# The top-32 threshold of attention rows from folded halves: scans of 288 columns in place of 576

## Chip, cores, metric

The kernel runs on one core of one Trainium2 chip. The time is that of the device in microseconds; three runs of the kernel before gave 2672.0, 2672.44 and 2674.5, median 2672.44.

## What is computed

Attention over 8 batches, 8 heads, 576 tokens and head width 64, in which each row of scores keeps only its 32 largest; then a mixture of experts (top 1 of 8) on the 4608 rows of 512.

```python
scores = scale * np.matmul(q, k.transpose(0, 1, 3, 2))
kth = np.partition(scores, -top_k, axis=-1)[..., -top_k:-top_k + 1]     # top_k = 32
scores = np.where(scores >= kth, scores, -1e9)
attn = np.exp(scores - np.max(scores, axis=-1, keepdims=True))
attn = attn / (np.sum(attn, axis=-1, keepdims=True) + 1e-09)
x = np.matmul(attn, v)                       # rows to (4608, 512)
expert_idx = np.argmax(x @ w_gate, axis=1)   # and its softmax weight gate_w
# rows sorted by expert:  y = relu(x @ w1[e]) @ w2[e];  out = gate_w * y
```

All data is float32.

## The kernel before

There are two stages. The first is attention with routing, the second the experts' blocks.

The first stage walks over 32 units (b, u): a batch and a pair of heads. A unit has nine score tiles of 128 query rows by 576 keys: four per head, and one that holds the last 64 rows of both heads. They are worked in five groups: `(i, NC + i)` for i = 0 to 3, which is the same rows of the two heads, and the ninth tile alone. For each tile `scores` makes 576 columns in two PSUM halves of 288 (PE, L182) and ACT copies them to `s` (L188; four buffers for all tiles). `weights` then finds the 32nd largest of each row on DVE: four times MAX8 (the eight largest of a row, L200) and between them three match_replace (L205), which overwrite those eight with -3e38. After the first MAX8, POOL makes `nbias` from the largest (L202) and ACT the exponentials `ex` (L203). One scalar_tensor_tensor (STT, L212) multiplies `ex` by `s >= 32nd value` into `w` (three buffers) and sums each row to `z`. `transposed` turns `w` on PE (L223, L224; the `wTl` tile has one PSUM buffer) and ACT copies the result to `wT`, `wTt` (L228, L229). When a unit's ninth tile is done, `outputs` multiplies by v in two halves of the queries (`po`, L253), ACT copies them to `oT` (L254), PE turns them back (`px`, `pl`), and DVE writes them, divided by `z`, into `x` (L262, L269; two buffers). After every eighth unit `route` finds the expert of 1152 tokens, writes their numbers to lists and `x` to `x_rows` in DRAM.

The code issues `scores` one group ahead of `weights`, and `finish` one tile behind. The order on each engine's queue is then chosen by a scheduler over the whole program; each engine works through its own queue in order, and a row that waits holds all behind it. In that order the scans of two neighbouring tiles are interleaved on DVE.

The second stage runs 25 blocks of 256 rows through the experts (L431 to L464). It doesn't depend on how the threshold was found.

Of the kernel before, what the change touches and what calls it, by code (L numbers as in the profile page):

```python
# [1 line left out]

# [28 lines left out]
def kernel(  # L31
# [9 lines left out]
):  # L41

# [90 lines left out]
    cnt = None  # L133
    firstp = ctx.enter_context(tc.tile_pool(name="firstp", bufs=1))
    first_w = None

    with (
        tc.tile_pool(name="pad", bufs=1) as padp,
        tc.tile_pool(name="load", bufs=2) as load,
        tc.tile_pool(name="att", bufs=2) as att,  # L140
        tc.tile_pool(name="wtp", bufs=2) as wtp,
        tc.tile_pool(name="xp", bufs=2) as xp,
        tc.tile_pool(name="small", bufs=3) as small,
        tc.tile_pool(name="ps_s", bufs=2, space=bass.MemoryType.PSUM) as ps_s,
        tc.tile_pool(name="ps_w", bufs=2, space=bass.MemoryType.PSUM) as ps_w,
        tc.tile_pool(name="ps_1", bufs=1, space=bass.MemoryType.PSUM) as ps_1,
    ):
        qk, vs_of, xt, units = {}, {}, {}, {}

        def load_qk(b, u):  # L150
            qb = load.tile([P, 2, S], F32, name="qb")
            nc.sync.dma_start(qb, qt[b, u * P:(u + 2) * P, :].rearrange("(u p) s -> p u s", p=P))
            kb = load.tile([P, 2, S], F32, name="kb")
            nc.sync.dma_start(kb, kt[b, u * P:(u + 2) * P, :].rearrange("(u p) s -> p u s", p=P))
            for n in range(2):
                qk[b, u + n] = (qb[:, n, :], kb[:, n, :])

        def load_v(b):
            vb = load.tile([P, KC, HD], F32, name="vb")
            nc.sync.dma_start(vb[:, 0:NC, :], vt[b, 0:SM, :].rearrange("(c p) d -> p c d", p=P))  # L160
            nc.sync.dma_start(vb[0:ST, NC, :], vt[b, SM:S, :])
            vs_of[b] = vb

        def parts(i):

            if i < 2 * NC:
                h, c = divmod(i, NC)
                return [(h, slice(0, P), slice(c * P, (c + 1) * P))]
            return [(h, slice(h * ST, (h + 1) * ST), slice(SM, S)) for h in range(2)]

        def scores(b, u, tiles):
            qu, ku = qk[b, u]
            todo = []
            got = []
            for i in tiles:
                ps = ps_s.tile([P, 2, SM], F32, name="sc")
                todo += [(ps, h, rows, cols) for h, rows, cols in parts(i)]
                got.append(ps)
            for j in range(2):
                for ps, h, rows, cols in todo:  # L180
                    d = slice(h * D, (h + 1) * D)
                    nc.tensor.matmul(  # L182
                        ps[rows, j, 0:HF], qu[d, cols], ku[d, j * HF:(j + 1) * HF], start=True, stop=True
                    )
            out_s = []
            for ps in got:
                s = att.tile([P, 2, HF], F32, name="s", bufs=4)
                nc.scalar.copy(s, ps[:, :, 0:HF])  # L188
                out_s.append(s)
            return out_s  # L190

        def weights(b, u, i, s3):
            s = s3[:, :, :].rearrange("p j k -> p (j k)")
            tops = small.tile([P, TOP_K // 8, 8], F32, name="tops")
            scr = att.tile([P, S], F32, name="scr")
            nbias = small.tile([P, 1], F32, name="nbias")
            ex = att.tile([P, S], F32, name="ex")
            src = s
            for r in range(TOP_K // 8):
                nc.vector.max(out=tops[:, r, :], in_=src)  # L200
                if r == 0:
                    nc.gpsimd.tensor_scalar(nbias, tops[:, 0, 0:1], -scale, None, ALU.mult)  # L202
                    nc.scalar.activation(ex, s, AF.Exp, scale=scale, bias=nbias)  # L203
                if r < TOP_K // 8 - 1:
                    nc.vector.match_replace(  # L205
                        out=scr, in_to_replace=tops[:, r, :], in_values=src, imm_value=NEG
                    )
                    src = scr
            w = att.tile([P, S], F32, name="w", bufs=3)
            z = units[b, u][2]  # L210
            c = 2 * NC if i == 2 * NC else 2 * (i % NC) + i // NC
            nc.vector.scalar_tensor_tensor(  # L212
                out=w, in0=s, scalar=tops[:, TOP_K // 8 - 1, 7:8], in1=ex,
                op0=ALU.is_ge, op1=ALU.mult, accum_out=z[:, c:c + 1],
            )
            return w

        def transposed(b, u, i, w):
            wT, wTt, _ = units[b, u]
            pm = ps_w.tile([P, NC, P], F32, name="wTm")  # L220
            pt = ps_1.tile([P, SM], F32, name="wTl")
            for c in range(NC):
                nc.tensor.transpose(pm[:, c, :], w[:, c * P:(c + 1) * P], ident)  # L223
# [291 lines left out]
```

## Time and profile before

| what | value |
|---|---|
| profiled execution | 2672.9 us, span 2671.2 us |
| PE busy | 2038.4 us (76%) |
| DVE busy | 1736.8 us (65%) |
| ACT busy | 718.1 us (27%) |
| POOL busy | 199.7 us (7%) |
| granted TensorE clock, mean | 0.719 of 2.4 GHz |

The shares are means over the two stages, which have different limits: in the first, to about 1850 us, DVE is the busiest engine, in the second PE. So they must be read by stage. A busy PE is counted from records whose ends are modelled; the time from one start to the next is surer. The clock is granted at two levels, 1.2 GHz (0.50) and 2.4 GHz (1.00); numbers between are means over a stretch.

### The profile page before, as it was taken

What the parts mean: (1) busy time and instruction counts of PE and PEld (TensorE: products, weight loads), DVE (VectorE), ACT (ScalarE), POOL (GpSimd) and SP (SyncE); (2) the same over time, 40 slices, a digit from 0 to 9 for tenths busy, and PEclk for the clock granted to TensorE, in tenths of its full rate; (3) what the DMA queues carried; (4) which work ended last, traced back from release to release, by engine and by line L of the source; (5) the groups of instructions that cost most, each with busy time, mean ns of one, the idle gap of its engine ahead of it and who ended that gap; (6) DMA issues with size and microseconds to landing.
All of it is one profiled execution on the core that took longest, in us unless ns stands there. A gap on an engine that the chain in (4) does not pass through costs nothing. (4 is left out here: it accounts for less than half of the span.)

```text
span 2671.2 us, 22208 instructions
## 1 busy us (share of the span) xinstructions
PE 2038.4 (76%) x7208; PEld 1205.5 (45%) x7208; DVE 1736.8 (65%) x3864; ACT 718.1 (27%) x1457; POOL 199.7 (7%) x453
## 2 busy tenths in 40 slices
PE   5766677666776876677686677676199999999998
PEld 3333344433333543333353333334166666666665
DVE  8999999699999869999986999995100010010000
ACT  3333333233333323333332333332011011001100
POOL 0000000100000010000001000000111111111110
PEclk8666656566656655655666656665599999999999
DMA  3000001100000110000011000000364444545440
GB/s 136 18 18 19 18 1 36 36 18 18 18 18 0 36 36 18 18 18 18 0 36 36 18 18 0 1 0 0 118 224 162 177 175 178 181 159 198 158 154 2
DMA packets 71172, 166.84 MB, mean 62 GB/s; under 512 B 9612, under 2 KB 9740, under 8 KB 71058
## 3 DMA queue, kind: packets, MB, share of 16 engines
q1 hardware_dynamic: 61906, 142.83, 15.8%
q0 software_dynamic: 9152, 22.60, 2.2%
q8 instruction: 58, 0.95, 0.1%
q14 instruction: 56, 0.46, 0.1%
HBM read 146.34 MB, written 22.73 MB: 63 GB/s over the span
## 5 line engine op out<-in xcount | busy, mean ns | idle before, releaser
L223 PE MATMUL wTm<-ident,w 128*128 128x128 f32 x1152 | 282.1, 392 | 490.1 <-DVE w L212 473.2
L200 DVE MAX8 tops<-scr 128x8 f32<-128x576 f32 x864 | 620.1, 744 | 0.5
L182 PE MATMUL sc<-kb,qb 64*128 64x288 f32 (+1 forms) x1280 | 575.2, 654 | 33.1 <-ACT s L188 26.0
L223 PEld LDWEIGHTS wTm<-ident,w 128*128 128x128 f32 x1152 | 187.7, 198 | 667.3 <-issue 498.9
L205 DVE MATCH_REPLACE8 scr<-tops,scr 128x576 f32<-128x576 f32 x576 | 424.9, 738 | 0.0
L182 PEld LDWEIGHTS sc<-kb,qb 64*128 64x128 f32 (+1 forms) x1280 | 279.2, 269 | 205.4 <-issue 109.7
L452 PE MATMUL ph<-xTs,w 128*128 128x256 f32 x1600 | 353.8, 382 | 14.1 <-DVE xTs L447 13.5
L188 ACT COPY s<-sc 128x576 f32<-128x576 f32 x288 | 184.3, 640 | 640.9 <-DVE w L212 632.7
L459 PE MATMUL py<-w,hT 128*128 128x512 f32 x800 | 347.4, 592 | 0.0
L452 PEld LDWEIGHTS ph<-xTs,w 128*128 128x128 f32 x1600 | 303.4, 191 | 60.4 <-DVE xTs L447 19.0
L463 DVE TENSOR_SCALAR y<-py,xg 128x512 f32<-128x512 f32 x50 | 37.5, 751 | 441.7 <-PE py L459 441.7
L253 PE MATMUL po<-wT,vb 128*64 128x288 f32 x1024 | 277.5, 642 | 1.4 <-ACT wT L228 0.9
L455 ACT ACTIVATE hT<-ph 128x256 f32<-128x256 f32 x200 | 76.8, 384 | 701.6 <-PE ph L452 701.6
L203 ACT ACTIVATE ex<-s,nbias 128x576 f32<-128x576 f32 x288 | 223.8, 777 | 94.0 <-POOL nbias L202 93.7
L459 PEld LDWEIGHTS py<-w,hT 128*128 128x128 f32 x800 | 152.0, 190 | 180.7 <-issue 179.4
L212 DVE SCALAR_TENSOR_TENSOR w<-s,tops,ex 128x576 f32<-128x576 f32 x288 | 230.1, 800 | 1.1 <-ACT ex L203 0.9
L200 DVE MAX8 tops<-s 128x8 f32<-128x576 f32 x288 | 213.7, 744 | 8.0 <-ACT s L188 7.9
L205 DVE MATCH_REPLACE8 scr<-tops,s 128x576 f32<-128x576 f32 x288 | 212.5, 738 | 0.0
L228 ACT COPY wT<-wTm 128x512 f32<-128x512 f32 x256 | 150.1, 586 | 171.3 <-PE wTm L223 168.1
L202 POOL TENSOR_SCALAR nbias<-tops 128x1 f32<-128x1 f32 x288 | 60.8, 211 | 1664.3 <-DVE tops L200 1393.5
L253 PEld LDWEIGHTS po<-wT,vb 128*64 128x64 f32 x1024 | 108.6, 213 | 163.4 <-issue 157.5
L431 DVE TENSOR_SCALAR src<-idx 128x2 int32<-128x2 int32 x25 | 4.2, 169 | 261.2 <-DMA idx<-lists 261.2
(89 smaller groups left out, 981.1 us busy)
## 6 DMA issues: line engine op xcount, KB each, us to landing
w<-in_moe_w_dram SPq DMA_DIRECT2D x50, 2048.0 KB, 11.2
qb<-in_qt_dram SPq DMA_DIRECT2D x16, 576.0 KB, 4.0
kb<-in_kt_dram SPq DMA_DIRECT2D x16, 576.0 KB, 4.9
x_rows<-x SPq DMA_DIRECT2D x8, 1026.0 KB, 10.7
vb<-in_vt_dram SPq DMA_DIRECT2D x8, 1024.0 KB, 5.9
x_rows<-x SPq DMA_DIRECT2D x8, 128.2 KB, 10.6
vb<-in_vt_dram SPq DMA_DIRECT2D x8, 128.0 KB, 6.1
xg<-x_rows,src POOLq DMA_INDIRECT x50, 7.7
```

The lines of the kernel that those rows point to most:

```text
L182: nc.tensor.matmul(ps[rows, j, 0:HF], qu[d, cols], ku[d, j * HF:(j + 1) * HF], start=True, stop=True)
L188: nc.scalar.copy(s, ps[:, :, 0:HF])
L200: nc.vector.max(out=tops[:, r, :], in_=src)
L203: nc.scalar.activation(ex, s, AF.Exp, scale=scale, bias=nbias)
L205: nc.vector.match_replace(out=scr, in_to_replace=tops[:, r, :], in_values=src, imm_value=NEG)
L212: nc.vector.scalar_tensor_tensor(out=w, in0=s, scalar=tops[:, TOP_K // 8 - 1, 7:8], in1=ex, op0=ALU.is_ge, op1=ALU.mult, accum_out=z[:, c: ...
L223: nc.tensor.transpose(pm[:, c, :], w[:, c * P:(c + 1) * P], ident)
L228: nc.scalar.copy(wT[:, :, h, q], pm)
L253: nc.tensor.matmul(po[rows, 0:HF], lhsT, rhs, start=(c == 0), stop=(c == KC - 1))
L452: nc.tensor.matmul(ph, w1[:, 0, dt, f * P:(f + 1) * P], xT[:, dt, :], start=(dt == 0), stop=(dt == DT - 1))
L455: nc.scalar.activation(hT[:, f, :], ph, AF.Relu)
L459: nc.tensor.matmul(py, hT[:, f, c * P:(c + 1) * P], w2[:, 0, f, :], start=(f == 0), stop=(f == FT - 1))
```

## The change

Columns j and j + 288 of a row of scores are taken as a pair. `hl[:, 0, :]` is the larger of each pair and `hl[:, 1, :]` the smaller, two tensor_tensor of 288 columns on DVE. The four MAX8 and three match_replace now run over the 288 larger ones; one more MAX8 takes the eight largest of the smaller ones. The 32nd value of the whole row is the largest of nine minima: the (32 - j)th larger one against the jth smaller one, j = 0 to 8, with 3e38 in place of the 0th. Two small operations per group (`both`, `thr`) do this. If the eighth smaller one reaches the threshold, more than eight might, and the result is in doubt: `over` (POOL) and `doubt` (DVE) record it, and at the end of the program a branch runs attention and experts once more with the old scans, if any row was in doubt.

Other edits: `weights` takes a group (two tiles) at once, with `tops` in four fixed tiles, four `ex` and three `scr` buffers; `finish` takes a group too; `x` has one buffer in place of two; the pad tile moves to another pool; helper functions move out of the `with` block.

```diff
     def scores(b, u, tiles):
...
             s = k.att.tile([P, 2, HF], F32, name="s", bufs=4)
             nc.scalar.copy(s, ps[:, :, 0:HF])
+            if not k.exact:
+                hl = k.att.tile([P, 2, HF], F32, name="hl", bufs=4)
+                nc.vector.tensor_tensor(hl[:, 0, :], s[:, 0, :], s[:, 1, :], op=ALU.max)
+                nc.vector.tensor_tensor(hl[:, 1, :], s[:, 0, :], s[:, 1, :], op=ALU.min)
...
-    def weights(b, u, i, s3):
+    def weights(b, u, tiles, ss):
...
+            src = [hl[:, 0, :] for _, hl in ss]
+            width = HF
+        scr = [k.att.tile([P, width], F32, name="scr", bufs=3) for _ in tiles]
         for r in range(R):
+            for m in range(n):
+                nc.vector.max(out=tops[:, m, r * 8:(r + 1) * 8], in_=src[m])
             if r == 0:
+                nc.gpsimd.tensor_scalar(nbias[:, 0:n], tops[:, 0:n, 0], -scale, None, ALU.mult)
+                for m in range(n):
+                    nc.scalar.activation(ex[m], s[m], AF.Exp, scale=scale, bias=nbias[:, m:m + 1])
+                if not k.exact:
+                    for m in range(n):
+                        nc.vector.max(out=tops[:, m, TOP_K + 1:TOP_K + 9], in_=ss[m][1][:, 1, :])
             if r < R - 1:
+                for m in range(n):
+                    nc.vector.match_replace(
+                        out=scr[m], in_to_replace=tops[:, m, r * 8:(r + 1) * 8],
+                        in_values=src[m], imm_value=NEG,
                     )
+                    src[m] = scr[m]
...
+            nc.vector.tensor_tensor(
+                both[:, 0:n, :], _back(tops[:, 0:n, TOP_K - 9:TOP_K]), tops[:, 0:n, TOP_K:TOP_K + 9], op=ALU.min
+            )
+            nc.vector.tensor_reduce(thr[:, 0:n], both[:, 0:n, :], axis=AX.X, op=ALU.max)
+            nc.gpsimd.tensor_tensor(over[:, c:c + n], tops[:, 0:n, TOP_K + 8], thr[:, 0:n], op=ALU.subtract)
...
+    again = nc.values_load(any_i[0:1, 0:1], min_val=0, max_val=P)
+    with tc.If(again > 0):
...
```

`_back` reverses the last axis of an access pattern. Two places of the order that the scheduler makes follow. In the names, a number is a buffer's, so that a copy and its reader can be matched.

The first place is DVE in the middle of a unit. Before, two tiles' scans and an STT:

```order
L200 MAX tops_1015<-s_955 128x8 [waits Pool_49]
L200 MAX tops_981<-scr_982 128x8 [waits DVE_49]
L205 MATCH_REPLACE scr_1016<-tops_1015,s_955 128x576 [waits DVE_49]
L205 MATCH_REPLACE scr_982<-tops_981,scr_982 128x576 [waits DVE_49]
L200 MAX tops_1015<-scr_1016 128x8 [waits DVE_49]
L200 MAX tops_981<-scr_982 128x8 [waits DVE_49]
L205 MATCH_REPLACE scr_1016<-tops_1015,scr_1016 128x576 [waits DVE_49]
L212 SCALAR_TENSOR_TENSOR w_994,z_730<-s_900,tops_981,ex_984 128x576 [waits DVE_49,PE_49,Activation_49]
L200 MAX tops_1015<-scr_1016 128x8 [waits DVE_49]
```

And now, after the two STT of a group:

```order
L252 MAX tops2_113<-hl_1661 128x8
L223 TENSOR_TENSOR hl_1723<-s_1721 128x288 [waits Activation_49]
L224 TENSOR_TENSOR hl_1723<-s_1721 128x288
L223 TENSOR_TENSOR hl_1728<-s_1726 128x288 [waits Activation_49]
L224 TENSOR_TENSOR hl_1728<-s_1726 128x288
L255 MATCH_REPLACE scr_1734<-tops2_113,hl_1656 128x288
L255 MATCH_REPLACE scr_1735<-tops2_113,hl_1661 128x288
L245 MAX tops2_113<-scr_1734 128x8 [waits DVE_49]
L245 MAX tops2_113<-scr_1735 128x8 [waits DVE_49]
L255 MATCH_REPLACE scr_1734<-tops2_113,scr_1734 128x288 [waits DVE_49]
```

Scans alternate between two tiles as before, now of half the width. The four tensor_tensor rows are new; they wait for ACT's copies `s` of the next group and stand ahead of the current group's first match_replace.

The second place is the end of a unit, where the first half of the outputs (`po`) is made. PE before:

```order
L182 MATMUL sc_1354<-kb_733,qb_731 128x288 [waits PE_49,Activation_49]
L182 MATMUL sc_1354<-kb_733,qb_731 128x288
L253 MATMUL po_1393<-wT_1039,vb_143 64x288 [waits Activation_49]
L253 MATMUL po_1393<-wT_1039,vb_143 64x288 x5
L223 MATMUL wTm_1300<-ident_62,w_1274 128x128 [waits DVE_49,PE_49]
L223 MATMUL wTm_1300<-ident_62,w_1274 128x128 x3
L224 MATMUL wTl_1301<-ident_62,w_1274 64x128 [waits Activation_49]
L182 MATMUL sc_1355<-kb_733,qb_731 128x288 [waits PE_49,Activation_49]
L182 MATMUL sc_1355<-kb_733,qb_731 128x288
L253 MATMUL po_1393<-wT_1039,vb_143 64x288
L253 MATMUL po_1393<-wTt_1040,vb_143 64x288 x2
```

PE now:

```order
L213 MATMUL sc_1844<-kb_838,qb_836 128x288 [waits PE_49]
L213 MATMUL sc_1844<-kb_838,qb_836 128x288
L213 MATMUL sc_1901<-kb_838,qb_836 128x288 [waits PE_49]
L213 MATMUL sc_1901<-kb_838,qb_836 128x288
L321 MATMUL po_1965<-wT_1539,vb_840 64x288 [waits DMAHW1_49]
L321 MATMUL po_1965<-wT_1539,vb_840 64x288 [waits Activation_49]
L321 MATMUL po_1965<-wT_1539,vb_840 64x288 x6
L321 MATMUL po_1965<-wTt_1540,vb_840 64x288 [waits DMAHW2_49]
L321 MATMUL po_1965<-wTt_1540,vb_840 64x288 [waits Activation_49]
L289 MATMUL wTm_1879<-ident_62,w_1821 128x128 [waits DVE_49,PE_49]
L289 MATMUL wTm_1879<-ident_62,w_1821 128x128 x3
L290 MATMUL wTl_1880<-ident_62,w_1821 64x128
```

Where `po` stood in pieces between the transposes of single tiles, four rows of scores (two tiles) and all of `po`'s half now stand together, ahead of the transposes of `w_1821`. ACT before at that place:

```order
L228 COPY wT_1039<-wTm_1300 128x4x128 [waits PE_49]
L229 COPY wTt_1040<-wTl_1301 64x128 [waits PE_49]
L203 ACTIVATE ex_1322<-s_1259,nbias_1321 128x576 [waits Pool_49]
L254 COPY oT_1392<-po_1393 128x288 [waits PE_49]
L188 COPY s_1360<-sc_1354 128x576 [waits DVE_49]
L228 COPY wT_1039<-wTm_1334 128x4x128 [waits PE_49]
L229 COPY wTt_1040<-wTl_1335 64x128 [waits PE_49]
```

ACT now:

```order
L249 ACTIVATE ex_1860<-s_1787,nbias_1859 128x576 [waits Activation_49,Pool_49]
L219 COPY s_1854<-sc_1844 128x576 [waits DVE_49,PE_49]
L294 COPY wT_1539<-wTm_1879 128x4x128 [waits PE_49]
L295 COPY wTt_1540<-wTl_1880 64x128 [waits PE_49]
L219 COPY s_1907<-sc_1901 128x576 [waits DVE_49]
```

The copy `s_1360` stood behind `oT`, the end of po's half; the copy `s_1907` stands ahead of `oT`, but behind the wT pair of `wTm_1879`, which is the transpose of `w_1821` and follows the same half of po on PE. And DVE now, from the STT that makes `w_1821`:

```order
L277 SCALAR_TENSOR_TENSOR w_1821,z_1541<-s_1721,thr_1818,ex_1793 128x576 [waits DVE_49,PE_49]
L277 SCALAR_TENSOR_TENSOR w_1823,z_1541<-s_1726,thr_1818,ex_1794 128x576 [waits PE_49]
L252 MAX tops0_109<-hl_1789 128x8
L223 TENSOR_TENSOR hl_1856<-s_1854 128x288 [waits Activation_49]
L224 TENSOR_TENSOR hl_1856<-s_1854 128x288
L255 MATCH_REPLACE scr_1861<-tops0_109,hl_1789 128x288 [waits DVE_49]
L223 TENSOR_TENSOR hl_1909<-s_1907 128x288 [waits Activation_49]
L245 MAX tops0_109<-scr_1861 128x8 [waits DVE_49]
```

The tensor_tensor that reads `s_1907` is the sixth row, and the single tile's MAX8 stands behind it.

## Rows read from the trace of the kernel before

**Rows 1.** The page's 40 slices: busy tenths of DVE and granted TensorE clock.
```profile
DVE  8999999699999869999986999995100010010000
PEclk8666656566656655655666656665599999999999
```

**Rows 2.** Windows of 100 us: busy us (instructions) by engine, granted clock, DMA share, GB/s.
```profile
800.00:900.00 100.00, 70.56 (x238) 37.23 (x237) 93.74 (x207) 34.24 (x68) 3.33 (x16) 0.60 0.04 12
...
2000.00:2100.00 100.00, 98.30 (x361) 66.36 (x361) 8.77 (x16) 11.34 (x30) 11.94 (x12) 1.00 0.49 175
```

**Rows 3.** DVE timeline, middle of a unit: start us, us, engine, line, operation.
```profile
403.99 0.81 DVE L212 SCALAR_TENSOR_TENSOR w<-s,tops,ex 128x576 f32<-128x576 f32 x1
404.72 0.76 DVE L200 MAX8 tops<-scr 128x8 f32<-128x576 f32 x1
405.39 0.74 DVE L200 MAX8 tops<-s 128x8 f32<-128x576 f32 x1
406.05 0.08 DVE L205 MATCH_VALUE_LOAD scr<-tops,scr 128x8 f32 x1
...
406.77 0.09 DVE L205 MATCH_VALUE_LOAD scr<-tops,s 128x8 f32 x1
```

**Rows 4.** DVE timeline, end of a unit and the same place a unit later.
```profile
387.49 0.80 DVE L212 SCALAR_TENSOR_TENSOR w<-s,tops,ex 128x576 f32<-128x576 f32 x1
...
397.38 0.69 DVE L262 TENSOR_TENSOR x<-px,rz 128x512 f32<-128x512 f32 x1 [3.03 <-PE px L261]
397.99 0.08 DVE L205 MATCH_VALUE_LOAD scr<-tops,scr 128x8 f32 x1
...
452.05 0.69 DVE L262 TENSOR_TENSOR x<-px,rz 128x512 f32<-128x512 f32 x1 [2.99 <-PE px L261]
```

**Rows 5.** Groups by shape, DVE and POOL: busy us, mean ns, idle before and its releaser.
```profile
L200 DVE MAX8 tops<-scr 128x8 f32<-128x576 f32 x864 | 620.1, 744 | 0.5
L205 DVE MATCH_REPLACE8 scr<-tops,scr 128x576 f32<-128x576 f32 x576 | 424.9, 738 | 0.0
L202 POOL TENSOR_SCALAR nbias<-tops 128x1 f32<-128x1 f32 x288 | 60.8, 211 | 1664.3 <-DVE tops L200 1393.5 <-ACT wT L228 213.6 <-ACT s L188 20.6
L311 DVE TENSOR_TENSOR base<-base,rank 128x8 f32<-128x8 f32 x36 | 5.5, 153 | 3.3 <-PE rank L304 3.0
```

**Rows 6.** Groups by shape, ACT.
```profile
L203 ACT ACTIVATE ex<-s,nbias 128x576 f32<-128x576 f32 x288 | 223.8, 777 | 94.0 <-POOL nbias L202 93.7
L188 ACT COPY s<-sc 128x576 f32<-128x576 f32 x288 | 184.3, 640 | 640.9 <-DVE w L212 632.7 <-PE sc L182 7.8
L228 ACT COPY wT<-wTm 128x512 f32<-128x512 f32 x256 | 150.1, 586 | 171.3 <-PE wTm L223 168.1
L229 ACT COPY wTt<-wTl 64x128 f32<-64x128 f32 x256 | 66.0, 258 | 8.2 <-PE wTl L224 8.2
```

**Rows 7.** PE timeline, end of a unit and one tile of two heads later.
```profile
388.45 1.08 PE L223 MATMUL wTm<-ident,w 128*128 128x128 f32 x4
389.67 2.29 PE L182 MATMUL sc<-kb,qb 64*128 64x288 f32 x4
391.89 3.67 PE L253 MATMUL po<-wT,vb 128*64 128x288 f32 x16
...
411.01 2.19 PE L182 MATMUL sc<-kb,qb 64*64 64x288 f32 x8
```

**Rows 8.** Windows of 2 us at the same place.
```profile
392.00:394.00 2.00, 2.00 (x10) 1.02 (x12) 2.00 (x4) 0.00 (x0) 0.00 (x0) 0.50 0.00 0
...
396.00:398.00 2.00, 1.50 (x12) 1.11 (x11) 0.62 (x2) 1.12 (x3) 0.00 (x0) 1.00 0.03 8
```

**Rows 9.** The page's DMA issues: the stores of x.
```profile
x_rows<-x SPq DMA_DIRECT2D x8, 1026.0 KB, 10.7
```

**Rows 10.** The instructions of L262 on DVE: duration ns, first and last start.
```profile
L262 DVE TENSOR_TENSOR x<-px,rz x32: 691/692/693, 73.3 to 1844.8; 128x512 f32<-128x512 f32 x32
```

**Rows 11.** The chain that ended last: start us, us, what.
```profile
2662.07 4.53 issue
```

More of the change, by code (lines that the diff above doesn't have):

```diff
@@ L111, with token_ids @@
     slots = iota_f("slots", [1, NSLOT], [[1, NSLOT]])
-    tok_id = []
-    for p in range(NP):
-        t = const.tile([P, NT], I32, name=f"tok_id{p}")
+    def token_ids(t, p):
         b0 = 2 * p * S
@@ L131, in load_w @@
         return w1, w2
-    cnt = None
     firstp = ctx.enter_context(tc.tile_pool(name="firstp", bufs=1))
[L135 to L183, printed above, removed]
-                    )
[L185 to L190, printed above, removed]
-        def weights(b, u, i, s3):
[L193 to L211, printed above, removed]
@@ new lines, with open_pools @@
+    groups = [(i, NC + i) for i in range(NC)] + [(2 * NC,)]
+    k = SimpleNamespace()
+    qk, vs_of, xt, units = {}, {}, {}, {}
+    def open_pools(st, load_bufs, exact):
+        for name, bufs in (
+            ("load", load_bufs), ("att", 2), ("wtp", 2), ("xp", 1), ("small", 3),
+        ):
+            setattr(k, name, st.enter_context(tc.tile_pool(name=name, bufs=bufs)))
+        for name, bufs in (("ps_s", 2), ("ps_w", 2), ("ps_1", 1)):
+            pool = tc.tile_pool(name=name, bufs=bufs, space=bass.MemoryType.PSUM)
+            setattr(k, name, st.enter_context(pool))
+        k.exact = exact
+        k.cnt = None
+        k.ntop = 0
+        k.late = None
@@ new lines, in weights, with transposed @@
+                out=w, in0=s[m], scalar=thr[:, m:m + 1], in1=ex[m],
+                op0=ALU.is_ge, op1=ALU.mult, accum_out=z[:, c + m:c + m + 1],
+            )
+            ws.append(w)
+        return ws
+    def transposed(b, u, i, w):
+        wT, wTt = units[b, u][0:2]
+        pm = k.ps_w.tile([P, NC, P], F32, name="wTm")
+        pt = k.ps_1.tile([P, SM], F32, name="wTl")
+        for c in range(NC):
+            nc.tensor.transpose(pm[:, c, :], w[:, c * P:(c + 1) * P], ident)
+        nc.tensor.transpose(pt[0:ST, 0:P], w[:, SM:S], ident)
+        if i < 2 * NC:
+            h, c = divmod(i, NC)
+            q = slice(c * P, (c + 1) * P)
+            nc.scalar.copy(wT[:, :, h, q], pm)
+            nc.scalar.copy(wTt[:, h, q], pt[0:ST, 0:P])
+        else:
+            nc.scalar.copy(wT[:, :, :, SM:S], pm[:, :, :].rearrange("p c (h q) -> p c h q", h=2))
+            nc.scalar.copy(wTt[:, :, SM:S], pt[0:ST, 0:P].rearrange("p (h q) -> p h q", h=2))
@@ L365, with close @@
         last = None
+        def close(last):
+            b, u, g, _ = last
+            finish(*last)
+            if g == groups[-1] and u == U - 1 and b % 2 == 1:
+                route(b // 2, tok_id[b // 2], (b - 1) * S)
         for n, (b, u, g) in enumerate(work):
             if g == groups[0]:
-                units[b, u] = (
-                    wtp.tile([P, NC, 2, S], F32, name="wT"),
-                    wtp.tile([ST, 2, S], F32, name="wTt"),
-                    small.tile([P, NT], F32, name="z", bufs=2),
-                )
+                open_unit(b, u)
@@ new lines @@
+            ws = weights(b, u, g, s_now)
+            if last is not None:
+                close(last)
+            last = (b, u, g, ws)
+        close(last)
+        slot_i = table(k.small, k.cnt)
+        any_p = k.small.tile([P, 1], F32, name="any_p", bufs=1)
+        nc.vector.tensor_reduce(any_p, doubt, axis=AX.X, op=ALU.max)
+        nc.vector.tensor_scalar(any_p, any_p, 0.0, None, ALU.is_ge)
+        pd = k.ps_1.tile([P, SM], F32, name="pd", tag="po")
+        nc.tensor.matmul(pd[0:1, 0:1], any_p, ones[:, 0:1], start=True, stop=True)
```

536 lines of the change are left out of this document (324 added, 212 removed).

## The prediction

> **What bounds the kernel now.** I read the 40 slices first, then a table of windows, then the DVE timeline inside one unit, then its neighbours PE and ACT at the unit's end. The slices show two stages [rows 1]: up to about slice 28 DVE is at 8 or 9 tenths under a TensorE clock of 5 to 6 tenths, and after that DVE falls to 1 or nothing and the clock stands at 9 (these are the MoE blocks). The windows say it with numbers [rows 2]: from 800 to 900 us DVE is busy 93.7 of 100, PE 70.6 at a granted clock of 0.60; from 2000 to 2100 PE is busy 98.3 and DVE 8.8 at clock 1.00. The change edits only the first stage, where DVE sets the pace.
>
> Inside that stage the unit of repetition is one (b, u): nine score tiles, then the outputs, 32 times. Two neighbouring `x<-px` multiplies, one per unit, start at 397.38 and 452.05: a unit takes 54.67 us, of which DVE waits 3.0 for PE's `px` and works 51.67 [rows 4]. Between, DVE runs without a gap: the start of a MAX8 follows the last MAX8 by 0.665 us, a match_replace with its value load takes 0.72, and the scalar_tensor_tensor (STT below) that compares with the 32nd value 0.73 [rows 3]. By hand: 36 MAX8 x 0.665 + 27 x 0.72 + 9 x 0.73 = 49.95 us; the other 1.7 of the 51.67 are the two x multiplies and the three small rz operations.
>
> **What the change does to DVE's work.** Per tile the four MAX8 and three match_replace of 576 columns become five MAX8 and three match_replace of 288, and two tensor_tensor (max, min) of 288 are new; the STT still covers 576. Per group there are two tiny operations more (`both`, `thr`), per unit one (`doubt`).
>
> How long a 288-column scan takes no row shows. I take the price of a column from the tensor_tensor rows: 153 ns at 8 columns [rows 5] and 0.69 us at 512 [rows 4] are 1.07 ns a column, so 288 columns fewer are 0.308 us fewer. Step from start to start: MAX8 0.665 - 0.308 = 0.357; match_replace 0.72 - 0.308 = 0.41. The tensor_tensor: the 512-column one hands over after 0.61 (397.38 to the next start at 397.99, in rows 4), so 0.61 - 224 x 1.07 ns = 0.37. Sum of a unit: 45 x 0.357 + 27 x 0.41 + 18 x 0.37 + 9 x 0.73 = 16.1 + 11.1 + 6.7 + 6.6 = 40.4; ten tiny operations at 0.09 and `doubt` 1.0; the old rest 1.7. Together 43.1 against 51.67: 8.6 us a unit less. Bounds: scans that halve completely (0.33 and 0.36) give 40.5; scans whose whole duration is exposed give 52.7 (worked out as a rival).
>
> DVE row: a MAX8 lasts 0.74 to 0.76 but the next one starts 0.67 later, so neighbours overlap by about 0.08 [rows 3]. The Trainium skill, page "VectorE: DVE Perf Modes", section "The DRAIN you can't avoid", says that, as a rule, after every VectorE operation the pipe is flushed before the next starts, and its advice is fewer operations rather than shorter ones. It speaks against this change, which has 10 large scans and element-wise operations per tile besides the STT where there were 7; by it each step would be a full duration and the unit's work 52.7 us. The trace does not agree: the 0.08 overlap is there at every step of the timeline, so I keep the smaller steps.
>
> **What becomes late next.** In the old order every DVE row reads what DVE made, or a score copy that has long been there. In the new one `hl` reads the copy `s` made by ACT one group ahead, and stands in DVE's queue in front of the current group's match_replace. `s` has four buffers, so the copy can start only after an STT of the group before has freed one.
>
> (1) Mid-unit, three times. After the second MAX8 of `hl` (0.44 long) come nbias on POOL (211 ns), two exps (777 ns each, in front of the copies in ACT's queue) and the first copy (640 ns) [rows 5, 6]: 0.44 + 0.1 + 0.21 + about 1.4 + 0.64 = 2.8 after that MAX8's start. DVE passes thr, a MAX8, two STT and a MAX8 in 2.6. Stall 0.2 each, 0.6 a unit.
>
> (2) At the unit's end, `hl` of the next unit's second group (the row that reads `s_1907` in the order shown with the change) waits for the copy `s_1907`. In ACT's queue that stands behind the wT copies of `w_1821`, whose transposes stand on PE behind two score tiles and a whole half of the outputs. Counted from the end of the second STT of the unit's third group: PE finishes that group's transposes and the wait for wTt by 2.1; two score tiles at 2.22 (389.67 to 391.89) make 6.5; the po half, 3.67 for 16 of its 20 instructions and so about 4.1, makes 10.6; four transposes 1.1 make 11.7 [rows 7]; wT and wTt copies 0.7 and the s copy 0.64 make 13.0 [rows 6]. DVE gets there after nine MAX8, seven match_replace, six tensor_tensor, two STT and two tiny ones, 3.2 + 2.9 + 2.2 + 1.5 + 0.2 = 10.0. Stall 3.0, if PE stays at its lower level, as it was at those rows (granted 0.50 of 2.4 GHz, [rows 8]).
>
> (3) `x<-px`: before, it started 9.9 us after the start of the last tile's STT (387.49 to 397.38) [rows 4]. That chain, transposes, wT copies, po, oT copy, px, is not touched; one score block in it is halved, so about 9.1. DVE now has seven MAX8, four match_replace, two tensor_tensor, three STT and 0.6 of small ones in front of it: 2.5 + 1.6 + 0.7 + 2.2 + 0.6 = 7.6. Stall 1.4, where 3.0 stood. (4) `x<-pl` now stands behind both STTs' transposes: 0.4.
>
> Sum: 43.1 + 0.6 + 3.0 + 1.4 + 0.4 = 48.5 us a unit, 6.17 less than 54.67. Of the 8.6 that DVE's work loses, 2.4 come back as waits.
>
> **Other edits.** ACT does the same copies and exps; a whole unit of them is about a third of the time [rows 2], hidden. PE has the same matmuls; one pair of score tiles per unit now alternates the two heads, and alternated blocks go faster (8 instructions in 2.19 at 411.01, against 4 in 2.29) [rows 7]: 2 us of PE per unit, off the path unless PE binds. The `over` subtractions on POOL, 160 of the kind of the 211 ns row [rows 5], lie beside DVE, since POOL is busy 3 of 100 [rows 2]; without that cover 34 us. x has one buffer in place of two: the first `x<-px` of a pair waits for four x_rows DMAs, 10.7 us to landing [rows 9], but it comes most of a unit after the routing that issues them: nothing, at most 3 x 10.7. Each routing costs (1844.8 - 73.3 - 31 x 54.67) / 3 = 25.6 us more than a unit [rows 4, 10], mostly PE; I leave it. The two branches and the test at the end: the nearest row is 4.53 us of issue at the end [rows 11]; I take 3, between 0 and 10. The MoE stage has the same instructions.
>
> **Sum.** 32 x 6.17 = 197 off, 3 on: 2672.9 - 194 = 2479. The profiled execution (2672.9) lies 0.5 above the median of 2672.44, inside the three runs' spread.
>
> **Rivals.** (A) the forecast, units of 47 to 50 us, 2431 to 2527: 0.56.
>
> (B) The stalls vanish. With less waiting PE may hold the upper clock level through the unit's end; then the two score tiles and the po half of (2) cost half, 4.3 less than above, and hardly more than (3) is left: unit 43.1 + 1.5 = 44.6, 32 x 10.07 = 322 off, 2354. For it: the granted clock goes from 0.50 at 392 to 1.00 at 396, while po runs behind transposes and scores without a gap [rows 7, 8], and in the new order more of PE's work stands together. Against: the whole stage has 5 to 6 tenths, so such spells are short [rows 1]. 0.15.
>
> (C) The loop DVE, ACT, PE binds more widely: every group's `hl` meets a copy that stands behind wT copies, 0.8 instead of 0.2 thrice and 4.7 instead of 3.0 at the end: unit 52, 32 x 2.67 = 85 off, 2591. For it: three in-order queues in one loop with four s buffers. 0.18.
>
> (D) Slower: PE becomes the bound at 1.2 GHz. A unit of PE at that level is nine tiles of scores at 2.22, 20, less 2 for the pair that alternates; nine tiles of transposes at 1.22, 11; two po halves, 8.2; px and pl, 1: 38.2 [rows 7]. Today PE idles 29.4 of 100, 16.1 us a unit [rows 2]. If those idles stay, because each group's transposes still wait for an STT, and the wait for wTt in (2), 2.1 - 1.2 = 0.9, comes in four groups, the unit is 38.2 + 16.1 + 3.6 = 57.9: 3.2 x 32 = 103 on and 3 for the end, 2779. It decides from PE idles above 16.5 us a unit at that clock. Against: the transposes of two tiles now come together, one idle where there were two. 0.04.
>
> (E) Short scans don't shrink, the DRAIN rule as a mechanism: step = duration. MAX8 0.744 - 0.308 = 0.436, match_replace 0.43 + 0.075, tensor_tensor 0.45, STT 0.88 [rows 3, 5]: 19.6 + 13.6 + 8.1 + 7.9, small ones 3.5, 52.7 a unit; with 2 of stalls 54.7: 2672.9 + 1 + 3 = 2677, no change. 0.05.
>
> (F) The flagged general path runs, and the time is above 4700. From the reference's inputs no row has more than six pairs with both scores in its top 32, where the flag needs eight, so 0.02.
>
> **From the cases.** A measurement of this kernel can tell about 0.2%, 5 us, from no change. Faster: A, B, C and 0.01 of E, 0.90; same: 0.03 of E; slower: D, F and the last 0.01 of E, 0.07. Range: it covers A, reaches to C's value and halfway to B's, 2388 to 2592; A's own is 2431 to 2527.
>
> **What would show it.** In the profile after: MAX8 of 288 columns with starts 0.35 to 0.37 apart and tensor_tensor at 0.37 (step E wrong if so); `x<-px` starts 48 to 49 us apart; DVE waiting on ACT's `s` for some 3.6 us a unit, most of it at one place at the end, and on `px` 1.4. If DVE's idle before `hl` is near nothing and the clock above 0.75 in the first stage, (B); if it stands at every group, (C); if PE is busy over 90 of 100 there, (D). The prediction is wrong if DVE's work a unit is not 42 to 45 us, or if the second stage is not 780 to 830 us as now.

## The result, and the profile after

The changed kernel takes 2406.98 us (median of 4 runs, 2398.49 to 2420.5) against 2672.22 of the kernel before beside it (2670.43 to 2674.5): a ratio of 0.901 [0.897, 0.905]. That is 9.9% faster, inside the predicted range and 72 us below the predicted 2479. The profiled execution took 2420.5 us (span 2418.8), the longest of the four; the comparison with [rows 1 to 11] is made by it.

The 40 slices again, busy tenths of DVE and the granted TensorE clock:

```profile
DVE  8899988799999699999769998930000010011000
PEclk9677766667766667676657767655999999999999
```

The first stage now ends in slice 27, of 60.5 us each, instead of slice 28, of 66.8 us each, and in it the clock shows 6 and 7 where it showed 5 and 6 [rows 1]. The multiplies `x<-px`, one a unit, then a window of 100 us without a routing (busy us of PE, PEld, DVE, ACT and POOL, then clock, DMA share, GB/s):

```profile
L330 DVE TENSOR_TENSOR x<-px,rz x32: 690/692/692, 68.9 to 1591.4; 128x512 f32<-128x512 f32 x32
```
```profile
1000.00:1100.00 100.00, 64.60 (x291) 36.48 (x289) 92.45 (x318) 41.20 (x85) 7.64 (x21) 0.73 0.08 24
```

The last one starts at 1591.4 instead of 1844.8 [rows 10]: 253.4 us earlier (4.4 of it already at the first one, 68.9 for 73.3), and the whole execution is 252.4 shorter. So everything lies in the first stage; from there to the end 827.4 us pass, and before it was 826.4. DVE stands at 92 of 100 there, as before [rows 2].

The groups by shape on DVE (busy us, mean ns, idle before and its releaser) show what the idle is now, and the last two lines what it was in the kernel before:

```profile
L245 DVE MAX8 tops<-scr 128x8 f32<-128x288 f32 x864 | 354.4, 446 | 0.1
L255 DVE MATCH_REPLACE8 scr<-tops,scr 128x288 f32<-128x288 f32 x576 | 251.4, 442 | 0.0
L277 DVE SCALAR_TENSOR_TENSOR w<-s,thr,ex 128x576 f32<-128x576 f32 x288 | 224.0, 809 | 0.4
L223 DVE TENSOR_TENSOR hl<-s 128x288 f32<-128x288 f32 x288 | 130.3, 452 | 79.2 <-ACT s L219 75.0
L330 DVE TENSOR_TENSOR x<-px,rz 128x512 f32<-128x512 f32 x32 | 22.1, 692 | 72.5 <-PE px L329 72.5
L358 DVE COPY lgs<-lg 128x72 f32<-128x72 f32 x4 | 0.9, 232 | 43.0 <-PE lg L354 43.0
```
```profile
L262 DVE TENSOR_TENSOR x<-px,rz 128x512 f32<-128x512 f32 x32 | 22.1, 692 | 120.4 <-PE px L261 120.3
L291 DVE COPY lgs<-lg 128x72 f32<-128x72 f32 x4 | 0.9, 232 | 78.1 <-PE lg L287 78.1
```

A MAX8 fell from 744 to 446 ns and a match_replace from 738 to 442 [rows 5]: 288 columns fewer are 298 ns, 1.035 ns a column. The new idle is that of `hl` for ACT's copy `s`, 75.0 us; `px` costs 72.5 where it cost 120.3, and `lg`, the logits of the routing, 43.0 where it cost 78.1. Of the 75.0 only 16.3 lie in the 27 units that hold no routing and are neither first nor last, 0.5 in most of them; 49 lie in the three units with a routing, and 9.5 ahead of the first `x<-px`.

Now one unit on DVE, from its first scans to its end (start us, us, line, operation, idle before):

```profile
212.07 0.69 DVE L330 TENSOR_TENSOR x<-px,rz 128x512 f32<-128x512 f32 x1 [3.10 <-PE px L329]
...
214.15 0.44 DVE L223 TENSOR_TENSOR hl<-s 128x288 f32<-128x288 f32 x1
214.51 0.44 DVE L224 TENSOR_TENSOR hl<-s 128x288 f32<-128x288 f32 x1
214.88 0.45 DVE L245 MAX8 tops<-hl 128x8 f32<-128x288 f32 x1
215.25 0.79 DVE L252 MAX8 tops<-hl 128x8 f32<-128x288 f32 x2
215.97 0.07 DVE L255 MATCH_VALUE_LOAD scr<-tops,hl 128x8 f32 x1
216.03 0.43 DVE L255 MATCH_REPLACE8 scr<-tops,hl 128x288 f32<-128x288 f32 x1
216.39 0.07 DVE L255 MATCH_VALUE_LOAD scr<-tops,hl 128x8 f32 x1
...
242.50 0.46 DVE L223 TENSOR_TENSOR hl<-s 128x288 f32<-128x288 f32 x1 [0.33 <-ACT s L219]
...
243.67 0.46 DVE L223 TENSOR_TENSOR hl<-s 128x288 f32<-128x288 f32 x1
...
248.79 0.81 DVE L277 SCALAR_TENSOR_TENSOR w<-s,thr,ex 128x576 f32<-128x576 f32 x1
...
259.84 0.69 DVE L330 TENSOR_TENSOR x<-px,rz 128x512 f32<-128x512 f32 x1 [3.10 <-PE px L329]
...
261.72 0.28 DVE L337 TENSOR_TENSOR x<-pl,rz 64x128 f32<-64x128 f32 x1 [0.45 <-PE pl L336]
```

From start to start the tensor_tensor step is 0.36 to 0.37, a MAX8 0.36 to 0.37, a match_replace with its load 0.42. The unit takes 259.84 - 212.07 = 47.77 us. Its waits in the whole timeline are 3.10 (`px`), 0.45 (`pl`), 0.33 and 0.16 (`hl`); 43.73 us are work, against 51.67 [rows 4]. This is one of the long units. Of the 27 ordinary ones (no routing, neither first nor last) 14 take 47.1 to 48.0, all but one of them with this wait of 3.1 for `px`, and 13 take 45.0 to 46.9, with a wait of at most 2.1; the mean of the 27 is 46.8, where it was 54.5 before. A unit with a routing takes 70.5 to 75.4.

PE in the second half of this unit (start us, us, line, operation, idle before), then three windows of 2 us:

```profile
235.04 2.30 PE L213 MATMUL sc<-kb,qb 64*128 64x288 f32 x8
237.27 2.20 PE L321 MATMUL po<-wT,vb 128*64 128x288 f32 x16
239.40 0.70 PE L321 MATMUL po<-wTt,vb 64*64 64x288 f32 x4
241.20 0.63 PE L289 MATMUL wTm<-ident,w 128*128 128x128 f32 x4 [1.10 <-DVE w L277]
...
249.75 1.09 PE L289 MATMUL wTm<-ident,w 128*128 128x128 f32 x4 [4.62 <-DVE w L277]
...
252.24 4.11 PE L321 MATMUL po<-wT,vb 128*64 128x288 f32 x16
256.28 1.23 PE L321 MATMUL po<-wTt,vb 64*64 64x288 f32 x4
257.43 1.32 PE L213 MATMUL sc<-kb,qb 64*128 64x288 f32 x2
258.69 1.11 PE L329 MATMUL px<-ident,oT 128*128 128x128 f32 x4
```
```profile
236.00:238.00 2.00, 2.00 (x12) 0.90 (x12) 2.00 (x9) 0.00 (x0) 0.00 (x0) 0.65 0.00 0
238.00:240.00 2.00, 2.00 (x18) 0.75 (x12) 2.00 (x8) 0.00 (x0) 0.00 (x0) 1.00 0.00 0
...
252.00:254.00 2.00, 2.00 (x9) 1.00 (x10) 2.00 (x8) 0.00 (x0) 0.00 (x0) 0.50 0.00 0
```

The two halves of the outputs are the same 20 matmuls. The first takes 2.8 us, because the clock is at 2.4 GHz from 238 on; the second, after PE had waited 4.62 us for `w`, takes 5.2 at 1.2 GHz, two more score rows and `px` itself (1.11) pass at that clock too, and `px` is late. Eight score matmuls of two neighbouring tiles, one of each head, passed in 2.30 us; four of one head took 2.29 [rows 7].

### The profile page after: what moved, and what is told of

The parts are those of the page before. It is cut to its first block, busy times and chain, and to the rows that moved or that the text cites. A ratio compares the mean times of both kernels' runs of the same rounds, so it can differ in the third digit from the quotient of the medians.

```text
span 2418.8 us, 23413 instructions
## 1 busy us (share of the span) xinstructions
PE 1781.4 (74%) x7210; PEld 1099.0 (45%) x7210; DVE 1487.1 (61%) x5087; ACT 694.8 (29%) x1457; POOL 257.2 (11%) x486
## 5 line engine op out<-in xcount | busy, mean ns | idle before, releaser
L289 PE MATMUL wTm<-ident,w 128*128 128x128 f32 x1152 | 265.7, 374 | 492.9 <-DVE w L277 490.6
L213 PE MATMUL sc<-kb,qb 64*128 64x288 f32 (+1 forms) x1280 | 401.7, 586 | 42.9 <-ACT s L219 35.8
L245 DVE MAX8 tops<-scr 128x8 f32<-128x288 f32 x864 | 354.4, 446 | 0.1
L213 PEld LDWEIGHTS sc<-kb,qb 64*128 64x128 f32 (+1 forms) x1280 | 185.8, 238 | 175.1 <-issue 96.8
L255 DVE MATCH_REPLACE8 scr<-tops,scr 128x288 f32<-128x288 f32 x576 | 251.4, 442 | 0.0
L277 DVE SCALAR_TENSOR_TENSOR w<-s,thr,ex 128x576 f32<-128x576 f32 x288 | 224.0, 809 | 0.4
L321 PE MATMUL po<-wT,vb 128*64 128x288 f32 x1024 | 205.8, 564 | 0.5 <-ACT wT L297 0.5
L223 DVE TENSOR_TENSOR hl<-s 128x288 f32<-128x288 f32 x288 | 130.3, 452 | 79.2 <-ACT s L219 75.0
L294 ACT COPY wT<-wTm 128x512 f32<-128x512 f32 x256 | 150.5, 588 | 28.7 <-PE wTm L289 27.5
L321 PEld LDWEIGHTS po<-wT,vb 128*64 128x64 f32 x1024 | 92.5, 188 | 118.3 <-issue 77.6
L247 POOL TENSOR_SCALAR nbias<-tops 128x2 f32<-128x2 f32 (+1 forms) x160 | 47.7, 298 | 818.5 <-DVE thr L271 440.4
L224 DVE TENSOR_TENSOR hl<-s 128x288 f32<-128x288 f32 x288 | 129.6, 450 | 0.0
```

The source lines that it names most:

```text
L213: nc.tensor.matmul(ps[rows, j, 0:HF], qu[d, cols], ku[d, j * HF:(j + 1) * HF], start=True, stop=True)
L223: nc.vector.tensor_tensor(hl[:, 0, :], s[:, 0, :], s[:, 1, :], op=ALU.max)
L245: nc.vector.max(out=tops[:, m, r * 8:(r + 1) * 8], in_=src[m])
L255: nc.vector.match_replace(out=scr[m], in_to_replace=tops[:, m, r * 8:(r + 1) * 8], in_values=src[m], imm_value=NEG,)
L277: nc.vector.scalar_tensor_tensor(out=w, in0=s[m], scalar=thr[:, m:m + 1], in1=ex[m], op0=ALU.is_ge, op1=ALU.mult, accum_out=z[:, c + m:c + ...
L321: nc.tensor.matmul(po[rows, 0:HF], lhsT, rhs, start=(c == 0), stop=(c == KC - 1))
```

## The experiments

The theory: the fold makes DVE's work shorter, the first stage goes at DVE's pace, and what it lacks to the full gain are waits in DVE's queue. Against it stand that the regrouping made the gain, and that PE or its clock sets the pace by now. Ratios are to the kernel before, run on the same chip in the same batch.

**Regrouping without the fold.**

```diff
-        open_pools(st, 2, False)
+        open_pools(st, 2, True)
```

> The changed kernel with the old scans of 576 columns in its first stage (no hl, both, thr, over); grouping, order, buffers and the branch at the end stay. Theory 1 (the fold's saving is DVE's own work, and the regrouping is worth nothing by itself): DVE's work a unit is back at 51 to 52 us and the time at 2650 to 2700 us. Rival (the regrouping, with two heads' scores next to each other on PE, carried a good part of the gain): 2600 or less. Other rival (the regrouping costs something that the fold pays for): 2730 or more.

Measured: 2659.65 us, 0.989 [0.987, 0.991]. Two neighbouring `x<-px`:

```profile
L330 DVE TENSOR_TENSOR x<-px,rz x2: 692/692/692, 348.9 to 403.0; 128x512 f32<-128x512 f32 x2
```

A unit of 54.1 us, nearly the old 54.67, and a time inside the expected 2650 to 2700. The regrouping, with the other buffers and the branch at the end, gives 1.1% by itself; the fold on top of it gives the other 8.8. The two are not a plain sum: the next run shows what the alternation that comes with the regrouping is worth once the fold is there.

**Both heads from the same rows.** All scores come from head 0's 64 rows of `qb` and `kb`, so the matmuls of two heads don't alternate between the halves of the 128 rows; head 1 gets head 0's scores.

```diff
-                d = slice(h * D, (h + 1) * D)
+                d = slice(0, D)
```

> The changed kernel, but both heads' scores read head 0's 64 rows of q and k, so that two score tiles can't use different row halves of PE at once; head 1's scores are therefore head 0's. Theory (the stall of 3.0 us that was forecast at the unit's end did not come because two tiles of different heads pass PE in the time of one): a pair takes 4.5 us again at the lower clock, DVE waits 2 to 3 us a unit for the score copy s, 64 to 96 us in all, 2470 to 2500. Rival (it did not come because the clock was higher there): within 1% of the changed kernel, 2385 to 2430.

Measured: 2466.81 us, 0.918 [0.916, 0.920]. PE and DVE at the place in the unit where the prediction had put its stall of 3.0:

```profile
333.14 4.21 PE L213 MATMUL sc<-kb,qb 64*128 64x288 f32 x8
337.27 4.11 PE L321 MATMUL po<-wT,vb 128*64 128x288 f32 x16
```
```profile
344.22 0.46 DVE L223 TENSOR_TENSOR hl<-s 128x288 f32<-128x288 f32 x1 [2.19 <-ACT s L219]
...
358.24 0.69 DVE L330 TENSOR_TENSOR x<-px,rz 128x512 f32<-128x512 f32 x1 [0.94 <-PE px L329]
```

Here is the predicted picture: two tiles in 4.21, the po half in 4.11 at the low clock, a stall of 2.19 (2.2 to 2.7 in most units) at the row where the changed kernel has none, and 0.94 left for `px` (1.4 predicted). DVE's wait for `s` rose from 75 to 145 us and that for `px` fell from 72 to 45, so the cost, 1.7% of the time before (0.918 less 0.901), is below what was expected. The alternation is what kept the stall away, but not by the scores alone: without it the scores took 1.9 us longer, and the po half stayed at the low clock and took 1.9 us longer too. The run doesn't part the two.

**Less DVE work.** The min, its MAX8 and so the smaller half of each pair are left out; the slots hold a constant.

```diff
-                nc.vector.tensor_tensor(hl[:, 1, :], s[:, 0, :], s[:, 1, :], op=ALU.min)
...
-                if not k.exact:
-                    for m in range(n):
-                        nc.vector.max(out=tops[:, m, TOP_K + 1:TOP_K + 9], in_=ss[m][1][:, 1, :])
```

> The changed kernel without the minimum of each pair and its MAX8 (the low values are taken as -3e38, so the threshold is that of the larger ones alone). DVE's work falls by 9 x (0.37 + 0.36) = 6.6 us a unit. Theory 1 (DVE's work still sets the unit): 211 us less, 2180 to 2215. Rival (the loop of PE, ACT and DVE is next to bind and gives a large part back as waits): less than 130 of the 211, 2280 or more, with DVE's waits for s or px up.

Measured: 2407.69 us, 0.896 [0.894, 0.897]. DVE was busy 209 us less (1278.4 for 1487.1), and the time hardly fell. Here the theory failed, and its rival came. The whole first stage (from the first `x<-px` to the last) and a window of it, then a wait:

```profile
60.42:1573.81 1513.39, 1130.07 (x4343) 621.09 (x4341) 1151.66 (x4169) 584.80 (x1202) 127.35 (x334) 0.66 0.07 21
300.00:400.00 100.00, 81.33 (x322) 47.21 (x321) 74.78 (x270) 38.42 (x78) 5.11 (x20) 0.65 0.07 24
```
```profile
320.94 0.46 DVE L224 TENSOR_TENSOR hl<-s 128x288 f32<-128x288 f32 x1 [5.04 <-ACT s L220]
```

In the window DVE is down to 75 of 100, PE up at 81 with the clock at 0.65, and the ordinary units take 45.6 to 46.4, or 53 to 56 right behind a routing. DVE's wait for `s` is 206 us. So the loop from DVE's `w` through PE and ACT back to `hl`, at the clock that PE had and in this order of the queues, stood only about a microsecond below the mean unit of the changed kernel. The edits below that move rows get under it.

**More PE work.** To see whether the clock is that bound, six transposes that nobody reads follow every score tile on PE; first on the changed kernel, then on the last experiment's (the smaller halves again left out).

```diff
+        if not k.exact:
+            for ps in got:
+                for j in range(2):
+                    for _ in range(3):
+                        nc.tensor.transpose(ps[:, j, HF:HF + P], ident, ident)
```

> The changed kernel with six unread transposes of the identity behind each score tile on PE (into unused columns of its PSUM tile), only to keep PE at work. Theory (the unit of 47.8 us with 3.1 us of waiting for px is the one in which PE's granted clock is 0.50 while it makes the second half of the outputs; kept at 1.00 the unit is 45): ordinary units 45 to 46, the first stage's clock above 0.75, ratio to the kernel before 0.885 to 0.895. Rival (the extra rows only stand in PE's way, the clock is not what sets the wait): units of 48 or more, ratio 0.905 to 0.93.

> The kernel without the low values (e3, whose unit stayed at 46 us although DVE's work fell to 37) with the same unread transposes on PE. Theory (what binds there is the loop over PE at its lower clock): unit 42 us or less, ratio 0.85 or less. Rival (the loop binds through the order of the queues and the ACT copies, not the clock): unit 45 to 47, ratio 0.885 or more.

Measured: 2530.32 us, 0.944 [0.941, 0.947], on the changed kernel, and 2199.39, 0.820 [0.815, 0.824], on the one with less DVE work. A window of each, the former first, then the whole first stage of the latter:

```profile
300.00:400.00 100.00, 76.98 (x377) 46.07 (x375) 88.08 (x306) 38.19 (x79) 6.00 (x20) 0.80 0.04 12
```
```profile
800.00:900.00 100.00, 89.18 (x494) 54.88 (x494) 99.46 (x360) 49.06 (x102) 10.08 (x27) 0.92 0.07 25
60.80:1363.94 1303.14, 1115.85 (x5985) 709.17 (x5983) 1151.15 (x4168) 587.54 (x1202) 127.81 (x334) 0.86 0.08 24
```

With less DVE work, more PE work took 208 us off: the clock over the stage is 0.86 instead of 0.66 (0.92 in the window), 17 of the 27 ordinary units take 37.0 to 37.3, and in the window, which holds such units, DVE is full. That settles that the bound of the kernel without the smaller halves was PE at its lower clock. On the changed kernel the same rows cost 4 to 5% (0.944 against 0.901, and 0.905 in its second measurement) although the clock rose to 0.80 in the window, and the time lies above both expectations. The extra rows stand in PE's queue ahead of what ACT copies, and `hl` waits for it. A wait of `hl`, then ACT's copy of the first po half in another long unit (the first) and in a short one (the second):

```profile
352.94 0.46 DVE L228 TENSOR_TENSOR hl<-s 128x288 f32<-128x288 f32 x1 [5.05 <-ACT s L224]
```
```profile
102.18 0.40 ACT L327 COPY oT<-po 128x288 f32<-128x288 f32 x1 [8.92 <-PE po L326]
148.96 0.40 ACT L327 COPY oT<-po 128x288 f32<-128x288 f32 x1 [5.39 <-PE po L326]
```

Of its 27 ordinary units 11 take 47.2 to 47.4 and 16 take 51.4 to 52.0. In the long one the scores, the extra rows and the po half took 11.4 us on PE, most of it at 0.50 (90.75 to 102.13); in the short one the same rows took 7.2 at 1.00 (141.76 to 148.91). The next copy `s` stands behind `oT` on ACT, and `hl` waited 5.04 for it in the one and 0.35 in the other. So the two lengths are the clock's, in that stretch; why it rose in some units and not in others was not settled.

**Waits moved in the queue.** Two edits move rows later without changing work. In the first the outputs of a unit (and the routing) come one group later; in a second form the routing is not moved.

```diff
-            finish(*last)
-            if g == groups[-1] and u == U - 1 and b % 2 == 1:
-                route(b // 2, tok_id[b // 2], (b - 1) * S)
+            for i, w in zip(g, ws):
+                transposed(b, u, i, w)
+            flush()
+            if g == groups[-1]:
+                k.late = (b, u)
...
+                outputs(b, u)
```

> The changed kernel with a unit's outputs (and the routing) issued one group later, so that x<-px stands later in DVE's queue. Theory (DVE waits for px only because the multiply stands too early in its queue): the 72 us of waits for px go almost all, 2330 to 2365. Rival (the wait only moves, to s, to w's transposes or to the routing): 2395 to 2425.

> The changed kernel with a unit's outputs one group later (e4), but not for the units ahead of a routing, whose outputs and routing come at once. Theory (e4 gained 1 to 3 us on ordinary units and lost about 11 us at each routing, since routing started a group later): both are had, ordinary units 44.3, routing units 72, ratio 0.873 to 0.880. Rival (the routing unit is long whatever the start, because DVE waits for PE's logits): 0.886 to 0.892 as e4.

Measured: 2388.28 us, 0.888 [0.887, 0.890], and 2384.15, 0.889 [0.887, 0.890]. In the first form:

```profile
L330 DVE TENSOR_TENSOR x<-px,rz 128x512 f32<-128x512 f32 x32 | 22.1, 692 | 7.6 <-PE px L329 6.6
...
L358 DVE COPY lgs<-lg 128x72 f32<-128x72 f32 x4 | 0.9, 232 | 80.9 <-PE lg L354 80.9
```

The wait for `px` is gone (6.6 us in all), ordinary units take 44.2, and routing units 83 to 88 instead of 70 to 75: 27 units gained 2.5 us each, 67 us, and three routings gave 37 of it back; `lg` is now waited for 80.9 us instead of 43.0. With the routing left in place the two units around one take about as long together, with the wait at `hl` (107.5 us in all) instead of `lg`. The waits for `px` went as the theory had it, but the routings took part back: the first form lies between its two expectations, and for the second the rival came.

The other edit issues max and min at the start of `weights`, right before their first reader, and not in `scores`, one group ahead.

```diff
-                nc.vector.tensor_tensor(hl[:, 0, :], s[:, 0, :], s[:, 1, :], op=ALU.max)
-                nc.vector.tensor_tensor(hl[:, 1, :], s[:, 0, :], s[:, 1, :], op=ALU.min)
...
+            for a, hl in ss:
+                nc.vector.tensor_tensor(hl[:, 0, :], a[:, 0, :], a[:, 1, :], op=ALU.max)
+                nc.vector.tensor_tensor(hl[:, 1, :], a[:, 0, :], a[:, 1, :], op=ALU.min)
```

> The changed kernel with max and min of the pairs issued with the scans that read them, not a group ahead. Theory 1 (the 75 us that DVE waits for s are lost because the fold stands ahead of ready work): they go, ratio 0.873 to 0.88. Rival (they are the wait for PE at the routing, which then shows up at another row): 0.895 to 0.908.

> The changed kernel with the fold issued with its scans (e8) and a unit's outputs and the routing one group later (e4). Theory (the two waits that are left add up, s in the unit's middle and px at its end, and both go): ordinary units 43.4 to 43.7, ratio 0.868 to 0.877. Rival (the routing unit takes back what the ordinary units gain, as in e4 and e7): 0.88 to 0.888.

Measured: 2367.83 us, 0.883 [0.881, 0.884], alone, and 2349.4, 0.874 [0.872, 0.876], with the outputs late too, the best of the kernels that leave nothing out. The two waits, with the fold late (and its `lg`), and with both late:

```profile
L231 DVE TENSOR_TENSOR hl<-s 128x288 f32<-128x288 f32 x288 | 127.7, 443 | 29.5 <-ACT s L219 29.5
L332 DVE TENSOR_TENSOR x<-px,rz 128x512 f32<-128x512 f32 x32 | 22.1, 692 | 50.4 <-PE px L331 50.4
L360 DVE COPY lgs<-lg 128x72 f32<-128x72 f32 x4 | 0.9, 233 | 68.6 <-PE lg L356 68.6
```
```profile
L231 DVE TENSOR_TENSOR hl<-s 128x288 f32<-128x288 f32 x288 | 127.3, 442 | 20.9 <-ACT s L219 20.6
L332 DVE TENSOR_TENSOR x<-px,rz 128x512 f32<-128x512 f32 x32 | 22.1, 692 | 8.4 <-PE px L331 7.5
```

The fold late alone came out between its theory and its rival. The wait for `s` at the routings did move on, to `lg` (68.6 for 43.0), and the routing units grew to 74 to 78. The gain lies in the ordinary units, 44.5 for 46.8 in the mean, where `hl` hardly had a wait to lose (0.5): `px` is now waited for about 1.0. PE there waits 0.5 to 3.3 for `w` before the second po half, where it waited 4.62 in the unit shown above, and in all 27 the clock rose within that half and `px` passed at the high clock. That one brought about the other was not tested.

With both, which came as expected, the ordinary unit is 43.3 to 43.6 us, about the work alone (43.73 in the changed kernel), so these units are at DVE's bound. What is left to gain there is DVE's work, and the routings' 79 to 82.

**The changed kernel again**, unedited, five runs.

> The changed kernel itself, beside e9 on one chip, to compare directly. By the first job: ratio 0.897 to 0.906, its runs spread over nearly 1%. If the two lengths of its unit (45 to 46 with the clock up, 47.8 with it down) come from how the granted clock falls, their mix is another one in this run's trace; if they belong to places in the program, the same units are long.

Measured: 2431.19 us (2418.12 to 2433.86), 0.905 [0.903, 0.906]. In its profile (span 2416.4) the ordinary units with 3.1 for `px` (47.2 to 48.0 us) stand at other places: 9 to 13, 22 and 30, where the first profile has 1 to 5, 18 to 19 and 25 to 30 (each numbered by the `x<-px` that starts it). In both profiles `px` took 1.11 us, the low clock, in each of them, and 0.66 in every other ordinary unit. The same code at the same place gave either length, so the length goes with the granted clock of that stretch, not with the place in the program.

## Why the prediction was right, and where its sizes were off

- DVE's work a unit: 43.1 predicted, 43.73 measured. The column price, 1.07 ns from two tensor_tensor rows, came out as 1.035, and each large step stands within 0.02 of its forecast. This mechanism was right and carries nearly the whole gain: 7.94 us less work a unit is about 246 us over 31 units, and between the first `x<-px` and the last DVE was busy 240.8 us less (1592.7 before, 1351.9 after).
- Rival E, steps as long as durations, is refuted: at 288 columns a MAX8 lasts 0.45 and the next starts after 0.36 to 0.37, so the overlap of 0.08 of [rows 3] stays. The Trainium skill's rule in "VectorE: DVE Perf Modes", "The DRAIN you can't avoid", that the next operation waits for the pipe to empty, doesn't show in either trace; the section itself adds that some next operations start earlier.
- The step that failed in size is "Of the 8.6 that DVE's work loses, 2.4 come back as waits". By it 77 us were to come back; DVE's waits in the stage are about 205 us now, and were about 211. They changed places and hardly their sum. In an ordinary unit they are 3.1 (46.8 less 43.7), about as before, and not 5.4. Its parts:
- Stall (1), 0.2 thrice: 0.16 and 0.33 in the unit shown. Stall (4), 0.4: 0.45.
- Stall (2), 3.0 for `hl` at the unit's end, was the mis-sized term: at the predicted place, the row at 243.67, no wait stands. Two tiles at 2.22 had been charged, 4.45 us, though the prediction itself noted that alternated blocks go faster, and called it off the path; they took 2.30. The po half was charged 4.1 at the low clock and took 2.8, since the clock rose in it. Together 3.4 us, more than the stall. With the alternation taken away the stall came, 2.19.
- Stall (3), 1.4 for `px`: 72.5 / 32 = 2.3 on average, 3.1 in the long units. There the chain from the last STT took 11.05 us (248.79 to 259.84), not 9.1. Before, PE ended it so:

```profile
395.49 0.70 PE L253 MATMUL po<-wTt,vb 64*64 64x288 f32 x4
396.69 0.66 PE L261 MATMUL px<-ident,oT 128*128 128x128 f32 x4 [0.50 <-ACT oT L254]
```

- The score block ahead of po was halved, as forecast, but two score rows now stand between po and `px`, 1.26 from start to start, where 0.50 of waiting stood. The second po half took 5.2 at the low clock, where it took 4.3 (391.89 to 396.19), and `px` 1.11 for 0.66. In the short units the wait is at most 2.1.
- Rival B, the stalls vanish as the clock rises, was half right: it names one of the two things that removed (2), the clock in the po half, and not the alternation. By its own sign the idle before `hl` is near nothing in an ordinary unit, but the stage's clock (from the first `x<-px` to the last) is 0.69, not above 0.75, and the waits for `px` stayed. The stage ended between A and B. Rivals C, D and F didn't come: a routing-free window shows DVE at 92 of 100, not PE.
- The end branch, 3 us assumed: the second stage and the end took 1.0 us more. The routings, left unchanged at 25.6 more than a unit: read from the units themselves they were 28.7 more before (the sum that gave 25.6 took the shorter first and last unit for whole ones), and are 25.7 and 28.2 in the two profiles of the changed kernel. What they hold changed: more of their wait is `hl`'s and less `lg`'s. The `over` subtractions, at most 34 us, took 72.6 on POOL, beside DVE as said.
- In sum 194 off were predicted and 252 came: 241 of DVE's work, 8 of its waits, 4 of an earlier first `x<-px`, less 1 at the end. The median lies another 13 below the profiled run, the longest of the four. Both lie below A's own range (2431 to 2527); the stated range held because it was drawn towards B.
- Two signs of the section "What would show it" failed with stall (2): the `x<-px` starts lie 45.0 to 48.0 apart and not 48 to 49, and the wait for `s` is 0.5 in an ordinary unit and not 3.6.

What was argued and not shown: why the clock is granted in one unit and not in the next with the same code.

## What to carry to other kernels

A scan that is made narrower is priced by the column from any element-wise row on the same engine, and step by step from starts, not from durations; that part of the forecast was good to 0.6 us in 44. What is late next must be priced at the rates that the new order gives (alternated tiles, the clock after the work just ahead), since two such rates decided here between a stall of 3.0 and none. Once the bounding engine is shorter, a row that waits should stand in its queue as late as its reader allows: two such moves were worth 2.7 to 3.1% of the time before (0.901 and 0.905 to 0.874) at no change of work. Part of a wait that is moved only goes on to the next row, as it did here at the routings.

## What the runs showed of the hardware that was not expected

- Two score tiles of different heads, on different halves of the 128 rows, pass PE in the time of one: 8 matmuls in 2.30 us, against 4.21 where both use the same half, all at the low clock or nearly so. The faster pass of the ninth tile had been read off before; that it decides a stall was not expected.
- More work made a kernel faster: in the one without the smaller halves, 1728 transposes that nobody reads took 2407.69 us to 2199.39 (two chips; 0.896 to 0.820 of the kernel before beside each), with the granted clock of the stage from 0.66 to 0.86. Where DVE had its whole work the same rows cost 4 to 5%.
- The changed kernel is less steady than the one before: its runs spread over 22 us of 2407 (0.9%), those of before over 4 us of 2672 (0.15%), and on another chip its median was 2431.19. Its ordinary units take 44.9 to 48.0 us in its two profiles. In both, units just ahead of a routing aside, the wait for `px` is 3.1 where the second po half and `px` ran at the low clock, 1.9 to 2.1 where only the po half did, and at most 1.3 where the clock rose within it.
